# Local attention over 17 blocks of 128 keys without padding, fewer projection units, products in six steps, a new order

## The chip, the cores and the metric

The kernel runs on one core of a Trainium2 chip. Its time is the device time of one execution in microseconds (us). TensorE (PE; its weight loads are listed apart as PEld), VectorE (DVE), ScalarE (ACT) and GpSimd (POOL) compute; SyncE (SP), POOL and ACT issue transfers. Matrix products land in PSUM, eight banks of 512 fp32 columns, from which only DVE and ACT copy ("evict").

## The reference

Two branches over 2048 positions of width 640 share the input x = A_q and are mixed by a gate:

```python
g = sigmoid((x * gate_w).sum(-1, keepdims=True))
a = x * (longconv(kv, ssm_k) + kv * ssm_D)   # kv = shortconv4(A_k, shift_k) * A_v; longconv by rfft of length 4096
q, k, v = split(x @ wqkv)                    # 32 heads of width 20
b = softmax(q . k[pos - 2*w], w = 0..7) @ v, then @ wo     # 8 keys, two positions apart
out = g * a + (1 - g) * b
```

In `b` a position attends to itself and seven earlier positions of the same parity. So even and odd positions are two independent sequences of 1024 ("halves"), each with a window of 8.

## The kernel before, in words

**Order.** Everything is written as generators ("streams") that yield requests for an engine. The string `ORDER` names, character by character, whose next request is granted, and a `-` before a letter takes the second of the engines that the request allows (of "AD": ACT without, DVE with it). `Steps.run` replays this string, so it fixes the order on each engine. PSUM is handed out in the same replay (four slots of two banks, or single banks as halves). Engines run their own instructions in order and wait for each other by semaphores.

**Attention, tiles.** `xpose` transposes x into `xT` (five tiles of 128 rows; even positions, then odd, each half with padding). `vproj` makes the values of one block (`VW`, 18 blocks: 9 in each half, 114 queries and 121 keys per block, since a block needs 7 earlier keys). `qkproj` makes the queries and keys of 128 features (`ft` = 0 to 4) of all positions in *units* of five matmuls, one per tile of `xT`, into a staging tile `stg`, whose key rows are written as overlapping blocks. `fragger` moves rows of `stg` by DMA to `kb` and `qb`: four heads lie at partitions 0, 32, 64, 96, and above each head's 20 rows stand 11 rows of numbers that drive every score outside the window far below zero (`attn_consts`, `masks`). The first seven query fragments are issued by SP ("near"), the others by POOL. `NSTG` = 2 staging tiles, one for queries and one for keys, are reused by the next `ft`. Sets of four heads, t0 to t7, use three `kb`/`qb` pairs. `score_gen` makes the scores of a set in five groups of blocks, ACT takes their exponential into `ETall` (two activations a group), and `pv_gen` multiplies by the values in two parts of a set; a column of ones gives the sum, DVE takes its reciprocal and multiplies. The result `oS` lies in `VW`'s memory; `op_tr` transposes it to `oT`, and `outproj` makes 16 x 2 groups `bl`, each scaled by 1-g when it is evicted.

**Convolution.** `conv` and `conv_v` (DVE) make kv. A transform of length 4096 in two steps of products is applied to the filter (`h_stream`: tile H for half P=0 of the channels, SX for P=1) and to kv (`u_stream`, tile UC): 10 groups of the first step (evictions of 1024), then 11 of the second (`JS`, evictions of 960, the last 640). `swaps` makes a copy Hw of the transformed filter with its rows exchanged: per P four pairs of DMAs on SP, where each pair waits for the one before by way of a small POOL copy. `products(P)` multiplies on DVE, 11 steps of two; `inverse1` (20 groups of 16 matmuls) waits for all products of its P; `final` makes six groups (`TAIL`, 96 or 64 matmuls) in PSUM, evicts each by two copies into `yb`, multiplies by x*g (`load_q` loads x again and scales it) and adds `bl`; then SP stores. `load_T` and `load_wo` bring constants and the last weights on SP.

Of the kernel before, what the change touches and what calls it, by code (L numbers as in the profile page):

```python
# [13 lines left out]
ALU = mybir.AluOpType  # L14
# [12 lines left out]
BQ = 114  # L27
BK = 121
NBP = 9
NB = 2 * NBP  # L30
PRE = 7
X0 = 16
HS = 1024
HP = HS + 16
XW = X0 + 2 * HP
NF = 11
NT = 8
QW = BQ * NB
KW = BK * NB
NET = 9  # L40
GROUPS = [[0, 1, 2, 3], [4, 5, 6, 7], [8, 9, 10, 11], [12, 13, 14], [15, 16, 17]]
# [49 lines left out]
def attn_consts():  # L91
    B, C = 256.0, 512.0
    kk = np.arange(BK); qq = np.arange(BQ)
    kc = kk // 8 - 8; ko = kk % 8; qc = qq // 8 - 8; qo = qq % 8
    sk = np.where(kc % 2 == 0, 1.0, -1.0); sq = np.where(qc % 2 == 0, 1.0, -1.0)
    mk = np.zeros((NF, BK)); mq = np.zeros((NF, BQ))
# [5 lines left out]
    tot = np.einsum("fk,fq->kq", mk, mq)  # L102
    dlt = kk[:, None] - qq[None, :]
# [112 lines left out]
def kernel(  # L216
# [80 lines left out]
    xT = pL.tile([128, NDT, XW], BF, name="xT")  # L297
# [163 lines left out]
    def xdeps(i0, i1):  # L461
        return [ev(f"xT{a}") for a in range(max(0, i0) // 128, (min(HS, i1) + 127) // 128)]
# [507 lines left out]
```

## Time and profile before

| | |
|---|---|
| runs | 223.54, 224.27, 224.25 us; median 224.25 |
| the profiled execution | 224.23 us, span of its instructions 222.5 us |
| busy | PE 204.3, PEld 165.8, DVE 185.0, ACT 174.9, POOL 51.1 us |
| mean granted TensorE clock | 0.991 |

A busy time is the time in which at least one instruction of an engine runs. Matmuls overlap, so a matmul's own duration is longer than the distance to the next; a rate is read from a row that holds many of them. Four engines are busy through most of the span, so what a saved instruction is worth depends on which engine ends last in its stage.

### The profile page before, as it was taken

The page shows a single profiled execution, that of the slowest core. Times are in us where ns is not written, and L with a number is a line of the kernel's source. Part 1 is how long each engine was busy: PE and PEld are TensorE (multiplying, and loading weights), DVE is VectorE, ACT ScalarE, POOL GpSimd, SP SyncE. Part 2 cuts the span into 40 slices and gives each one's busy share as a digit, 9 for nine tenths or more (in the row PEclk, how much of TensorE's full clock was granted, in tenths as well). Part 3 has the DMA queues.
Part 4 walks back from the last instruction along what each step waited for, and adds up shares of the span by engine and source line. Part 5 has one row for each costly group of instructions (what it writes and reads, how often), then busy time and mean ns, then how long its engine had stood idle before and what let it go on. Part 6 is the DMA issues. An engine that isn't in the chain of part 4 may idle for free.

```text
span 222.5 us, 8401 instructions
## 1 busy us (share of the span) xinstructions
PE 204.3 (92%) x3577; PEld 165.8 (75%) x3577; DVE 185.0 (83%) x261; ACT 174.9 (79%) x253; POOL 51.1 (23%) x129
## 2 busy tenths in 40 slices
PE   7999999999999999699997867999999999979990
PEld 3777987696777577466685756889888899979880
DVE  4745778997998898569898978998999997859992
ACT  0264487769998898599999988998999999478770
POOL 7980711470617044402450000000000000000000
PEclk9999999999999999999999699999999999999999
DMA  6999789599999999803993396678567082003645
GB/s 199 349 237 275 188 180 205 133 168 149 208 182 197 163 151 155 140 4 52 183 171 74 85 214 152 172 174 213 122 142 227 4 184 55 3 3 91 152 106 136
DMA packets 69049, 33.35 MB, mean 150 GB/s; under 512 B 51476, under 2 KB 66708, under 8 KB 69012
## 3 DMA queue, kind: packets, MB, share of 16 engines
q1 hardware_dynamic: 65684, 27.66, 61.3%
q0 software_dynamic: 2880, 4.90, 9.9%
q8 instruction: 28, 0.46, 1.0%
q10 hardware_dynamic: 448, 0.26, 0.4%
q14 instruction: 9, 0.07, 0.1%
HBM read 19.51 MB, written 2.62 MB: 100 GB/s over the span
## 4 chain that ended last, share of the span: by engine, by line
PE 51%; DVE 20%; ACT 10%; DMA 8%; issue 7%; POOL 2%; DVEq 0%; POOLq 0%; ACTq 0%
PE PS L568 14%; PE PS L521 8%; ACT ETall L650 6%; PE PS L835 6%; DMA kb<-stg 6%; DVE UC L245 5%; PE PS L869 4%; PE PS L724 4%; PE PS L674 3%; DVE SX L245 3%; PE PS L642 3%; DVE q L926 2%; DVE yb L245 2%; ACT H L243 2%; DVE q L924 2%
## 5 line engine op out<-in xcount | busy, mean ns | idle before, releaser
L650 ACT ACTIVATE ETall<-PS 121x912 bf16<-121x912 f32 (+1 forms) x80 | 63.8, 864 | 8.1 <-PE PS L642 7.7
L568 PE MATMUL PS<-xT,Wqk 128*128 128x342 bf16 (+1 forms) x300 | 49.7, 310 | 0.6 <-ACT stg L243 0.3
L243 ACT CAST UC<-PS 128x1024 bf16<-128x1024 f32 (+2 forms) x49 | 44.4, 1030 | 4.0 <-DVE UC L245 3.1
L568 PEld LDWEIGHTS <-Wqk 128*128 128x128 bf16 x300 | 27.4, 97 | 14.3 <-issue 0.5
L521 PE MATMUL PS<-WvT,xT 128*121 128x320 bf16 x180 | 27.5, 300 | 0.1
L467 DVE TENSOR_TENSOR KX<-KX 128x1280 bf16<-128x1280 bf16 x32 | 25.3, 820 | 0.3
L618 POOL DMA_DIRECT2D qb<-stg x29 | 14.6, 506 | 45.8 <-ACT stg L243 30.5
L869 PE MATMUL PS<-wo,oT 128*128 128x320 bf16 x160 | 24.4, 302 | 0.1
L521 PEld LDWEIGHTS <-xT 128*121 128x121 bf16 x180 | 23.4, 134 | 1.4
L243 ACT CAST stg<-PS 128x363 bf16<-128x363 f32 (+1 forms) x39 | 17.1, 471 | 7.8 <-PE PS L568 7.5
L869 PEld LDWEIGHTS <-oT 128*128 128x128 bf16 x160 | 21.1, 145 | 1.5 <-issue 0.5
L724 PEld LDWEIGHTS <-G 64*128 64x128 bf16 x512 | 18.2, 93 | 4.9 <-issue 3.7
L618 POOL DMA_DIRECT2D kb<-stg x36 | 18.1, 511 | 15.8 <-ACT stg L243 7.6
L642 PE MATMUL PS<-qb,kb 31*128 31x114 bf16 x576 | 16.0, 212 | 5.1 <-DMA kb<-stg 2.3
L245 DVE CAST stg<-PS 128x342 bf16<-128x342 f32 (+1 forms) x21 | 11.0, 522 | 11.7 <-PE PS L568 9.4
L642 PEld LDWEIGHTS <-kb 31*128 31x128 bf16 x576 | 9.4, 93 | 13.5 <-issue 9.8
L674 PEld LDWEIGHTS <-ETall 121*128 121x128 bf16 x576 | 17.4, 96 | 2.1 <-issue 0.5
L674 PE MATMUL PS<-VW,ETall 121*128 121x63 bf16 (+2 forms) x576 | 18.2, 184 | 0.6 <-DVE SX L245 0.3
L835 PE MATMUL PS<-F,Hw 128*128 128x128 bf16 x160 | 18.1, 219 | 0.0
L874 ACT ACTIVATE bl<-PS,omg 128x320 bf16<-128x320 f32 x31 | 16.1, 566 | 2.4 <-PE PS L869 1.9
L835 PEld LDWEIGHTS <-Hw 128*128 128x128 bf16 x160 | 17.9, 114 | 0.0
L245 DVE CAST UC<-PS 128x1024 bf16<-128x1024 f32 x13 | 15.3, 1219 | 2.6 <-ACT UC L243 1.2
(75 smaller groups left out, 334.1 us busy)
## 6 DMA issues: line engine op xcount, KB each, us to landing
xn<-in_A_q_dram SPq DMA_DIRECT2D x8, 320.0 KB
h_lin<-in_A_ssm_k_dram SPq DMA_DIRECT2D x16, 160.0 KB
vin<-in_A_v_dram SPq DMA_DIRECT2D x8, 320.0 KB
Hw<-H SPq DMA_DIRECT2D x8, 320.0 KB
q<-in_A_q_dram SPq DMA_DIRECT2D x8, 320.0 KB
Hw<-SX SPq DMA_DIRECT2D x8, 320.0 KB
kb<-stg POOLq DMA_DIRECT2D x28, 85.1 KB, 5.5
out_dram<-q SPq DMA_DIRECT2D x16, 120.0 KB
```

What stands on the lines that cost most here:

```text
L243: nc.scalar.copy(dst, src)
L245: nc.vector.tensor_copy(dst, src)
L467: eng.tensor_tensor(d, kin[:, n + 3 - j:n + 3 - j + m, :], w.to_broadcast([128, m, QC]), ALU.mult)
L521: nc.tensor.matmul(ps[0:BK, 0:320], lhsT=xT[:, dt, s0:s0 + BK], rhs=Wv[:, dt, 320 * hp:320 * hp + 320], start=(dt == 0), stop=(dt == NDT - 1))
L568: nc.tensor.matmul(ps[:, 0:n], lhsT=Wqk[:, dt, w, 128 * ft:128 * ft + 128], rhs=xT[:, dt, s0:s0 + n], start=(dt == 0), stop=(dt == NDT - 1))
L618: (nc.sync if near else nc.gpsimd).dma_start(dst[r0:r0 + rows, 0:wd], stg[fa - f0:fb - f0, 0:wd])
L642: nc.tensor.matmul(psum(g, h4 // 2)[:, h4 % 2, BQ * bb:BQ * bb + BQ], lhsT=kb[r:r + DH + NF, BK * b:BK * b + 128], rhs=qb[r:r + DH + NF, B ...
L650: nc.scalar.activation(ETall[0:BK, e, :, 0:BQ * nb], psum(g, k)[0:BK, :, 0:BQ * nb], ACT.Exp, scale=SCALE)
L674: nc.tensor.matmul(O[:, (b - b0) // 6, c0:c0 + 21 * nh], lhsT=ETall[0:BK, e, hh, BQ * bb:BQ * bb + 128], rhs=VW[0:BK, b, 4 * t + h4:4 * t ...
L724: nc.tensor.matmul(ps[:, c, 160 * jj:160 * jj + 160], lhsT=G[rows, j0 + jj, 64 - 64 * rr:192 - 64 * rr], rhs=Am[rows, rr].rearrange("p o ( ...
L835: nc.tensor.matmul(d, lhsT=st[(key, P)][:, c, o + il // 4, :, il % 4], rhs=M[:, k, :], start=(k == 0), stop=(k == 1), skip_group_check=True)
L869: nc.tensor.matmul(op, lhsT=oT[:, ft].rearrange("p h m a -> p a (h m)")[:, t, :], rhs=wo[:, ft, 320 * n:320 * n + 320], start=(ft == 0), s ...
```

## The change

- Attention uses 17 blocks of 128 keys over the positions of both halves put end to end, without padding (2048 columns of `xT`, before 2096). A block has 120 queries, or 128 at the start of each half; block 8 crosses from the even half to the odd one, for which the mask has a form of its own, as it has for the first block. A set's last group of blocks has 2 instead of 3. `vproj` makes 17 units instead of 18, of 128 keys.
- Query units are 4 of 512 positions, key units 5 of 488 or 368, in place of 6 + 6 of 342 and 349 for each `ft`: 45 units instead of 60. A query fragment's DMA now writes each row in two pieces of 1024 elements, since `qb` has 8 columns between the halves; key fragments stay in one piece.
- `masks` takes four POOL copies a set instead of two and a memset; memsets of padding go.
- `op_tr` transposes block 8 in two pieces (18 transposes a tile, as before).
- `products` takes six steps of two instead of eleven, with 1920 elements in place of 960.
- Scaling x by g may be done by ACT too, and `final` waits for each scaled tile by itself.
- `ORDER` is another one.

```diff
-BQ = 114
-BK = 121
-NBP = 9
-NB = 2 * NBP
+BQ = 120
+BK = 128
+NB = 17
...
-GROUPS = [[0, 1, 2, 3], [4, 5, 6, 7], [8, 9, 10, 11], [12, 13, 14], [15, 16, 17]]
+GROUPS = [[0, 1, 2, 3], [4, 5, 6, 7], [8, 9, 10, 11], [12, 13, 14], [15, 16]]
+QB = [(0, 128)] + [(BQ * b + 8, BQ) for b in range(1, 8)] + [(968, 128)] + [(BQ * b + 16, BQ) for b in range(9, NB)]
+KCH = [(0, 4), (10, 3), (4, 3), (7, 3), (13, 4)]
...
 ORDER = """
-a-aa-aw-wa-aw-ww-wiiai-iiaaiaa-aia-iii-aiaa-ii-iiii-ii-iiiicifffccccw-wwww-wwwwfwwwwf-wffffwwwwwwcwcccccwwwdw-wdwddddi-wfccccccii
+a-aa-awa-a-wwww-wwwa-awaii-waiiaaa-aaaiiiiiiiiif-iiffff-iiw-wiwwwicxf-wwwwwwwwwwwwwwfxffffffcccwccwcccccc-wccffdddii-iiiidcccccccc
...
 def masks(e):
-        nc.gpsimd.memset(ksets[e][:, KW:], 0.0)
-        nc.gpsimd.tensor_copy(ksets[e][:, 0:KW].rearrange("p (b k) -> p b k", k=BK), mm[:, 0:BK].unsqueeze(1).to_broadcast([128, NB, BK]))
-        nc.gpsimd.tensor_copy(qsets[e][:].rearrange("p (b k) -> p b k", k=BQ), mm[:, BK:BK + BQ].unsqueeze(1).to_broadcast([128, NB, BQ]))
+        k_, q_ = ksets[e][:], qsets[e][:]
+        nc.gpsimd.tensor_copy(k_.rearrange("p (b k) -> p b k", k=BK), mm[:, 0:128].unsqueeze(1).to_broadcast([128, NB, BK]))
+        nc.gpsimd.tensor_copy(raw(k_, 0, [k_.ap[0], [8 * BK, 2], [1, BK]]), mm[:, 128:384].rearrange("p (a k) -> p a k", a=2))
...
 def qkproj():
-            wd, n = (BK, BQ * 3 + PRE) if w else (BQ, BQ * 3)
+            s0, n = (BQ * KCH[k][0], BQ * KCH[k][1] + 8) if w else (512 * QCH[k], 512)
+            m = BK * KCH[k][1] if w else n
...
 def fragger():
-                    g = yield Req("S", 450.0, deps, move=28.0 * rows)
+                    g = yield Req("S", 740.0, deps, move=28.0 * rows)
...
-                (nc.sync if near else nc.gpsimd).dma_start(dst[r0:r0 + rows, 0:wd], stg[fa - f0:fb - f0, 0:wd])
+                to, src = dst[r0:r0 + rows], stg[fa - f0:fb - f0]
+                if w:
+                    (nc.sync if near else nc.gpsimd).dma_start(to[:, 0:KW], src[:, 0:KW])
+                else:
+                    (nc.sync if near else nc.gpsimd).dma_start(raw(to, 0, [to.ap[0], [HS + 8, 2], [1, HS]]), src[:, 0:2 * HS].rearrange("p (a n) -> p a n", a=2))
...
+    PG = [(0, 2), (2, 4), (4, 6), (6, 8), (8, 10), (10, 11)]
...
 def products(P):
-        for k, (j0, n) in enumerate(JS):
+        for k0, k1 in PG:
+            j0 = JS[k0][0]
+            n = sum(JS[k][1] for k in range(k0, k1))
             for key in "hw":
-                r = yield Req("D", 68.0 + 0.521 * 320 * n, [ev(f"todo{P}{k}"), ev(f"hw{P}")])
+                r = yield Req("D", 68.0 + 0.521 * 320 * n, [ev(f"todo{P}{k}") for k in range(k0, k1)] + [ev(f"hw{P}")])
...
 def load_q(half):
-            r = yield Req("D", 297.0, [Ev(r.done.src, 4500.0), ev("gate")] if t == 0 else [])
-            nc.vector.tensor_scalar(q[:, t], q[:, t], g_nat[:, 8 * half + t:8 * half + t + 1], None, ALU.mult)
+            r = yield Req("DA", dict(D=297.0, A=620.0), [Ev(r.done.src, 4500.0), ev("gate")] if t == 0 else [])
+            sc = g_nat[:, 8 * half + t:8 * half + t + 1]
+            if r.eng == "A":
+                nc.scalar.activation(q[:, t], q[:, t], ACT.Copy, scale=sc)
+            else:
+                nc.vector.tensor_scalar(q[:, t], q[:, t], sc, None, ALU.mult)
```

Three places show what the new order moves. The first is ACT from the first eviction of the kv transform (UC, 128x2x512, its first step; 128x80x12 and 128x80x8 are its second) towards the first eviction of `inverse1` (128x128x8). Before:

```order
L243 CAST UC<-PS 128x2x512 x12
L243 CAST UC<-PS 128x80x12 x11
L874 ACTIVATE bl<-PS,omg 128x320 x2
L243 CAST UC<-PS 128x80x12 x3
L874 ACTIVATE bl<-PS,omg 128x320 x4
L243 CAST UC<-PS 128x80x8
L243 CAST UC<-PS 128x80x12 x2
L874 ACTIVATE bl<-PS,omg 128x320 x3
L243 CAST UC<-PS 128x80x12 x2
L874 ACTIVATE bl<-PS,omg 128x320 x2
L243 CAST UC<-PS 128x128x8
```

and ACT at the same place now:

```order
L242 CAST UC<-PS 128x2x512 x9
L242 CAST UC<-PS 128x80x12 x2
L242 CAST UC<-PS 128x2x512 x3
L242 COPY oT<-PS 128x64x2x16 x2
L242 CAST UC<-PS 128x80x12 x3
L879 ACTIVATE bl<-PS,omg 128x320
L242 CAST UC<-PS 128x80x12 x3
L879 ACTIVATE bl<-PS,omg 128x320
L242 CAST UC<-PS 128x80x12 x2
L242 CAST UC<-PS 128x80x8
L879 ACTIVATE bl<-PS,omg 128x320 x4
L242 CAST UC<-PS 128x80x12 x2
```

ACT now takes two of the five `oT` copies that were DVE's, and DVE takes five second-step evictions that were ACT's; up to the first 128x128x8 eviction ACT has 15 of 960 and two of 640 (before 18 and one) and 10 of `bl` (before 11).

The second place is DVE in the last stage, from `final`'s first group on (yb: its evictions; q: x scaled by g, the two numbers are the two halves of the positions). Before:

```order
L245 CAST yb_3616<-PS 128x2x3x160
L924 TENSOR_TENSOR q_2391<-yb_3616,q_2391 128x1920
L890 TENSOR_SCALAR q_3452<-q_3452,g_nat 128x640 x2
L926 TENSOR_TENSOR q_2391<-q_2391,bl 128x1920
L890 TENSOR_SCALAR q_3452<-q_3452,g_nat 128x640
L245 CAST yb_3616<-PS 128x2x3x160
L924 TENSOR_TENSOR q_2391<-yb_3616,q_2391 128x1920
L926 TENSOR_TENSOR q_2391<-q_2391,bl 128x1920
L890 TENSOR_SCALAR q_3452<-q_3452,g_nat 128x640 x3
L876 TENSOR_SCALAR bl<-PS,omg 128x320
```

and DVE there now:

```order
L881 TENSOR_SCALAR bl<-PS,omg 128x320
L937 TENSOR_TENSOR q_2251<-yb_3446,q_2251 128x1920
L939 TENSOR_TENSOR q_2251<-q_2251,bl 128x1920
L881 TENSOR_SCALAR bl<-PS,omg 128x320 x2
L937 TENSOR_TENSOR q_2251<-yb_3446,q_2251 128x1920
L939 TENSOR_TENSOR q_2251<-q_2251,bl 128x1920
L937 TENSOR_TENSOR q_2251<-yb_3446,q_2251 128x1280
L939 TENSOR_TENSOR q_2251<-q_2251,bl 128x1280
```

All 16 scalings now stand ahead of `final` (12 on DVE, 4 on ACT), and 11 of the 12 `yb` copies are ACT's. On PE, 75 `outproj` matmuls now stand between the first and the last group of `final`, before 95; behind the last group stand 15, before 10; and between the first group of `inverse1` and `final` stand 15 in place of 32 smaller ones of the kv transform (its second step).

The third place is SP from the first swap on (Hw; H is the filter of P=0, SX of P=1; `SX<-cf_T` is `load_T`). Before:

```order
L820 DMA Hw<-H_294 64x5x512 x2
L886 DMA q_2391<-in_A_q_dram 32x8x640
L820 DMA Hw<-H_294 64x5x512 x2
L886 DMA q_2391<-in_A_q_dram 32x8x640
L820 DMA Hw<-H_294 64x5x512 x2
L886 DMA q_2391<-in_A_q_dram 32x8x640
L820 DMA Hw<-H_294 64x5x512 x2
L820 DMA Hw<-SX 64x5x512 x2
L323 DMA wo<-in_B_wo_dram 128x5x640
L820 DMA Hw<-SX 64x5x512 x6
L323 DMA SX<-cf_T 128x4x512 x2
```

and SP there now:

```order
L322 DMA SX<-cf_T 128x4x512
L825 DMA Hw<-H_281 64x5x512 x2
L322 DMA wo<-in_B_wo_dram 128x5x640
L891 DMA q_2251<-in_A_q_dram 32x8x640 x2
L825 DMA Hw<-H_281 64x5x512 x4
L322 DMA SX<-cf_T 128x4x512
L825 DMA Hw<-H_281 64x5x512 x2
L825 DMA Hw<-SX 64x5x512 x8
L891 DMA q_2251<-in_A_q_dram 32x8x640 x2
L891 DMA q_3215<-in_A_q_dram 32x8x640 x4
```

The loads of constants and of `wo` now stand among the swaps of P=0, those of P=1 follow each other without a load between.

More of the change, by code (lines that the diff above doesn't have):

```diff
@@ L461, in xdeps @@
     def xdeps(i0, i1):
[L462 removed]
+        return [ev(f"xT{a}") for a in sorted({i // 128 % 8 for i in range(i0, i1)})]
     def taps(eng, n, m, t3, dst):
@@ L585, in qkproj @@
         for ft in range(NDT):
-            for n in range(6):
-                g = yield from unit(ft, *((n % 2, n // 2) if ft == 0 else (n // 3, n % 3)))
+            for w, k in UFIRST if ft == 0 else [(w, k) for w in range(2) for k in range(5 if w else 4)]:
+                g = yield from unit(ft, w, k)
         mark("qk", g)
```

166 lines of the change are left out of this document (83 added, 83 removed).

## The prediction, made before the change was run

> **What bounds the kernel now.** I read the page's busy times first, then cut the span at landmarks of the order.
>
> ```profile
> PE 204.3 (92%) x3577; PEld 165.8 (75%) x3577; DVE 185.0 (83%) x261; ACT 174.9 (79%) x253; POOL 51.1 (23%) x129
> ```
>
> The cuts: first transpose, first scores of t4 and t6, first `u_stream` group, first `inverse1` group, first `final` group.
>
> ```profile
> core 0: us, PE busy (x) PEld busy (x) DVE busy (x) ACT busy (x) POOL busy (x), PEclk, DMA share, GB/s
> 4.57:93.46 88.89, 86.09 (x1159) 65.44 (x1158) 71.62 (x110) 63.76 (x104) 39.95 (x97) 1.00 1.04 195
> 93.46:118.95 25.49, 24.43 (x498) 17.63 (x499) 21.34 (x28) 23.73 (x34) 7.00 (x14) 1.00 0.56 102
> 118.95:143.03 24.08, 18.84 (x496) 15.48 (x496) 20.17 (x25) 22.39 (x29) 0.57 (x3) 0.93 0.65 143
> 143.03:175.70 32.67, 32.12 (x452) 28.90 (x450) 31.47 (x43) 31.73 (x41) 0.56 (x3) 1.00 0.61 156
> 175.70:196.22 20.52, 19.38 (x356) 19.08 (x353) 17.58 (x31) 17.40 (x21) 0.00 (x0) 1.00 0.32 66
> 196.22:222.50 26.28, 20.44 (x617) 18.25 (x616) 20.23 (x26) 15.88 (x27) 0.00 (x0) 0.99 0.41 103
> ```
>
> Five stages have five different states. Up to t4 PE ends last (86.1 of 88.9; DVE 72, ACT 64). Between t4 and t6 PE and ACT are both full. Then ACT leads (22.4 of 24.1, PE 18.8). From `u_stream` on PE, DVE and ACT all fill 31 to 32 of 32.7. The last two stages are PE's, with DVE close behind and the stores at the end.
>
> **Prices on PE.** The chain of waits shows gapless runs (start, length, matmuls):
>
> ```profile
> 17.68 4.43 PE PS L568 x30
> 22.12 8.15 PE PS L521 x60
> 30.27 0.32 PE PS L642 x16
> 37.33 1.30 PE PS L674 x48
> 177.97 11.75 PE PS L835 x208
> ```
>
> A matmul of 349 columns takes 147.7 ns, one of 128 takes 56.5 ns: 0.413 ns a column and 3.7 ns fixed. A value matmul takes 136 ns, a score 20, a value product 27. Projections have 300 matmuls of 103650 columns before and 225 of 103200 now: 450 x 0.413 + 75 x 3.7 ns = 0.46 us saved. Values: 10 x 136 ns = 1.36. Scores: 32 x 20 ns = 0.64 (nothing, if their 120 to 128 columns in place of 114 cost in proportion). Value products: 32 x 27 ns = 0.87. In all 3.3 us of PE, 1.5 of it ahead of t4: there stand four fifths of the projections (0.37), one value unit of the two (0.68), and half of scores and products (0.32 and 0.43), less 0.3 for a longer first unit of `ft` 4.
>
> **Waits on fragments.** PE stops twice at scores whose key fragments are still under way:
>
> ```profile
> PE PS L642 <- DMA kb<-stg: 2.3, 2, 1.9
> 74.99 0.38 PE L642 MATMUL PS<-qb,kb 31*128 31x114 bf16 x13 [0.38 <-DMA kb<-stg]
> 91.31 0.23 PE L642 MATMUL PS<-qb,kb 31*128 31x114 bf16 x3
> 93.46 0.38 PE L642 MATMUL PS<-qb,kb 31*128 31x114 bf16 x13 [1.92 <-DMA kb<-stg]
> 87.78 5.66 DMA kb<-stg
> ```
>
> The fragment (5.66 us) cannot start before the last key unit of its `ft` is evicted, so the wait is what PE's work between that unit and the scores fails to cover. Ahead of t4 the order now has one value unit more (0.68), a query unit of 512 columns for one of 342 (0.35) and four value products fewer (0.11): 0.9 us more cover. Ahead of t3 it has one value unit, 20 value products, 12 scores and 8 filter products more and two query units of 512 for four of 342 (0.7 less): some 1.0 more. So 0.4 goes wholly and 1.0 of 1.9, rounded: 1.4 us. Bounds: 0 (the longer key unit of 488 columns and its eviction come later) to 2.3 (both gone). **Start to t4: -1.5 - 1.4 = -2.9.**
>
> **t4 to u_stream.** PE sheds 1.6 more before t6, but ACT is busy 23.7 of 25.5 there and its exponentials hold the same elements (4112 columns a set, before 4104). I take -0.4; bounds 0 and -1.6. From t6 on ACT gets one more eviction (640 of SX, DVE's before) and DVE sheds it: +0.3, bounds -0.3 and +0.7.
>
> **u_stream to final.** What ACT and DVE take apiece:
>
> ```profile
> 11.81 1.23 ACT L243 COPY xT<-PS 128x1280 bf16<-128x1280 bf16 x1
> 143.78 11.24 ACT L243 CAST UC<-PS 128x1024 bf16<-128x1024 f32 x12
> 155.83 9.87 ACT L243 CAST UC<-PS 128x960 bf16<-128x960 f32 x11 [0.81 <-ACT UC L243]
> 165.55 0.98 ACT L874 ACTIVATE bl<-PS,omg 128x320 bf16<-128x320 f32 x2
> 154.53 2.35 DVE L245 COPY oT<-PS 128x2048 bf16<-128x2048 bf16 x2
> 158.91 0.65 DVE L756 TENSOR_TENSOR Hw<-UC,Hw 128x960 bf16<-128x960 bf16 x1
> 159.48 0.65 DVE L756 TENSOR_TENSOR H<-UC,H 128x960 bf16<-128x960 bf16 x1
> 202.81 1.16 DVE L924 TENSOR_TENSOR q<-yb,q 128x1920 bf16<-128x1920 bf16 x1
> 115.62 4.35 DVE L245 CAST H<-PS 128x960 bf16<-128x960 f32 x4
> 172.39 0.48 DVE L756 TENSOR_TENSOR Hw<-UC,Hw 128x640 bf16<-128x640 bf16 x1
> ```
>
> An `oT` copy of 2048 on ACT is not in the trace: 1.23 us (the 1280 copy) and 1.97 (in proportion) bound it; I take 1.9, since the large evictions above go nearly in proportion (0.94 us for 1024). Up to the first `inverse1` eviction ACT gains two of these (3.8) and a 640 (0.6) and loses three of 960 (2.7) and one `bl` (0.5): +1.2. On DVE products of 960 follow each other at 0.57 us; a multiplication of 1920 takes 1.16 where one of 960 takes 0.65, so 0.51 more: 1.08 each, 20 x (2 x 0.57 - 1.08) = 1.2 us saved over both P (bounds: 0 at 1.14 each, 3 if the whole 0.15 us that lies beyond 960 x 0.53 ns went each time). Five evictions of 960 (1.09 each) come in, two `oT` copies (1.17) go. P=0's products, the wait that the new six steps could make longer, thus end 2 to 3 us later against `u_stream`'s start (5.4 - 2.3 - 0.6, and a `bl`); now they end at 172.9, 2.8 ahead of the first `inverse1` group. So ACT sets it: **+1.2**, bounds 0 and +2.1 (ACT's and DVE's growth on one path). Between `inverse1` and `final` PE has 15 `outproj` matmuls (2.2, from the row below) in place of 32 of the transform (1.3): **+0.9**. The scalings moved ahead lie there beside PE's 18 us of `inverse1`.
>
> **The tail.**
>
> ```profile
> 196.22 1.02 PE L912 MATMUL PS<-UC,SX 32*32 32x160 bf16 x96 [1.14 <-ACT UC L243]
> 197.17 2.94 PE L869 MATMUL PS<-wo,oT 128*128 128x320 bf16 x20
> 214.39 0.76 PE L912 MATMUL PS<-UC,SX 32*32 32x160 bf16 x64
> 217.46 0.83 DVE L926 TENSOR_TENSOR q<-q,bl 128x1280 bf16<-128x1280 bf16 x1
> ```
>
> PE goes through `final` and `outproj` without a pause, so 20 fewer of the latter between first and last group, at 0.145 us (2.87 for 20), are **-2.9**. ACT must then evict two `yb` and two `bl` per round, 2 x 0.9 + 2 x 0.5 = 2.8 of PE's 3.2 us; that just fits (bound: 0.5 lost). DVE is relieved of scalings and copies. Behind the last group PE now has 15 matmuls: 0.7 + 2.2 + an eviction 0.5 + the add 0.8 and two handovers of 0.15 make 4.5 us to the end of the last add, before 3.9 (214.39 to 218.29): **+0.6**, bounds 0.3 and 0.9.
>
> Sum: -2.9 - 0.4 + 0.3 + 1.2 + 0.9 - 2.9 + 0.6 = -3.2. The profiled execution's 224.23 us (span 222.5 and 1.7 around it; the median is 224.25) becomes **221.0**. With every bound at its better end it is -1.5 - 2.3 - 1.6 - 0.3 + 0 + 0.9 - 2.9 + 0.3 = -7.4 (216.8), at its worse end -1.2 + 0 + 0 + 0.7 + 2.1 + 0.9 - 2.4 + 0.9 = +1.0 (225.2).
>
> **Free, and why.** Mask copies on POOL (some +1 us) end well ahead of the first fragment, DVE's shorter memsets lie before its first copy waits for PE, and the two pieces of block 8 keep 18 transposes.
>
> **Rivals.** *PE is no bound, no change (0.14).* By the prices above ACT and DVE together keep their work within 1 us (what fewer units save, `oT` and scalings give back on ACT, which is slower at them), and PEld is busy only 65 of 89 us ahead of t4. If PE only looks full, -3.3 there and the covers are worth nothing, and the tail's -2.3 pays for the middle's +2.1 and +0.3: 224.3. Against it: the gapless runs above go at a fixed price per column, so PE streams. The Trainium skill says so as a rule ("Perfetto Trace Analysis", Identifying the Most-Contended Engine): matmul busy time is a bad measure of PE, weight-load share a better one. By that rule PE has a quarter in hand here and the sum would be this rival's; the row of 349 columns at 147.7 ns speaks against it.
>
> *Query fragments in two pieces, slower (0.12).*
>
> ```profile
> 21.33 5.85 SPq L618 DMA_DIRECT2D qb<-stg  x7
> 26.52 0.67 SPq L618 DMA_DIRECT2D qb<-stg  x1
> L618 POOL DMA_DIRECT2D qb<-stg x29: 499/501/533, 38.2 to 107.5; - x29
> ```
>
> SP issues seven at 0.84 us, and t0's scores follow at 30.3. If a row in two pieces costs twice at SP, t0's four fragments leave 3.3 us later; the order starts those scores 2.3 us of PE work later, while the last query unit ends some 1.5 us later, so 2.5 us of wait remain; if the landing (5.66 above) doubled too, 8, and the time is 229. It turns slower from 4.3 us on. Against it: on POOL 4 rows cost what 20 do (499 to 533 ns), and on SP the 8-row fragment, 0.67, is near the mean.
>
> *Swaps come late (0.06).* Some 1500 KB more stand ahead of P=0's last swap:
>
> ```profile
> 127.31 1.25 SPq L820 DMA_DIRECT2D Hw<-H  x2
> 144.31 8.33 DVE L245 CAST UC<-PS 128x1024 bf16<-128x1024 f32 x7
> 134.01 0.19 POOL L814 COPY Hw<-Hw 128x1 bf16<-128x1 bf16 x1 [8.48 <-DMA Hw<-H]
> 139.48 0.19 POOL L814 COPY Hw<-Hw 128x1 bf16<-128x1 bf16 x1 [5.28 <-DMA Hw<-H]
> 139.70 1.25 SPq L820 DMA_DIRECT2D Hw<-H  x2
> ```
>
> A pair takes 5.3 to 6.7 us, the longer with 320 KB beside it, so 1500 KB cost up to 6.6. The last pair lands near 145; the first product now stands behind seven of these evictions and two of 960, so at 144.31 + 8.33 + 2.2 = 154.8 in this trace's time (before: 158.3). Only beyond 9.8 us is each paid in full; twice the price gives 224.4.
>
> *More gain (0.13).* Both waits go and PE's saving counts up to t6: -2.3 for -1.4 and -1.6 for -0.4, 218.9.
>
> **Chances.** Forecast 0.55 (219.3 to 222.8), the rivals as given. 0.5% (1.1 us) is about what can be told from no change. Faster 0.72: forecast, more gain and a part of the late swaps; same 0.16: mostly the first rival; slower 0.12. The range 217.0 to 224.8 leaves out most of the second rival and the far end of the last.
>
> **What would show it.** PE's waits on `kb` at most 1 us, no new wait at t0; t4's first score 2 to 3.5 us earlier, the first `u_stream` group at about 140, `final` at about 195, its last group 16 us later; products 1.07 us apart; POOL's query issue still 0.5 us. A PE wait of over 2 us anywhere, or ACT rounds longer than PE's in the tail, would make it wrong.

## The result and the profile after: slower by 3%

The changed kernel takes 231.47 us (229.56 to 231.84), the kernel before 223.89 in the same comparison: a ratio of 1.032 (95% interval 1.026 to 1.039). The forecast was 221.0 us, range 217.0 to 224.8. Medians and ratios here and below leave out executions more than 1.5% above the fastest of their kernel, and the profiles of experiments 5, 7 and 9 are of executions left out in this way. The kernel before was run again on the chip of each group of experiments (medians 225.24, 224.46, 224.73 and 224.81).

First the profiled execution of the changed kernel (229.56 us, the shortest of four): the page's busy times, then the same cuts as before at its own landmarks (first transpose, first scores of t4 and t6, first group of the kv transform, of `inverse1`, of `final`).

```profile
PE 205.6 (90%) x3418; PEld 153.5 (67%) x3428; DVE 181.6 (80%) x233; ACT 175.5 (77%) x242; POOL 55.7 (25%) x129
```

```profile
core 0: us, PE busy (x) PEld busy (x) DVE busy (x) ACT busy (x) POOL busy (x), PEclk, DMA share, GB/s
4.56:94.95 90.39, 85.00 (x1051) 52.63 (x1057) 68.47 (x101) 61.23 (x93) 43.15 (x93) 0.98 1.06 191
94.95:119.57 24.62, 22.84 (x465) 15.39 (x467) 22.80 (x29) 23.78 (x34) 8.59 (x23) 1.00 0.64 129
119.57:146.91 27.34, 22.24 (x481) 17.97 (x480) 20.08 (x26) 23.16 (x29) 0.57 (x3) 0.69 0.67 161
146.91:180.77 33.86, 33.35 (x483) 30.10 (x482) 32.32 (x32) 32.70 (x41) 1.02 (x3) 1.00 0.48 107
180.77:202.48 21.71, 20.12 (x339) 20.00 (x336) 19.69 (x28) 20.00 (x25) 0.00 (x0) 1.00 0.31 63
202.48:227.50 25.02, 19.06 (x602) 16.36 (x601) 16.66 (x19) 14.58 (x23) 0.00 (x0) 1.00 0.42 107
```

| stage | before | after | change | forecast |
|---|---|---|---|---|
| start to t4 | 88.89 | 90.39 | +1.5 | -2.9 |
| t4 to t6 | 25.49 | 24.62 | -0.9 | -0.4 |
| t6 to the kv transform | 24.08 | 27.34 | +3.3 | +0.3 |
| to `inverse1` | 32.67 | 33.86 | +1.2 | +1.2 |
| to `final` | 20.52 | 21.71 | +1.2 | +0.9 |
| `final` to the end | 26.28 | 25.02 | -1.3 | -2.3 |

Four stages came out within about 1 us of the forecast. Two did not, and they hold 7.4 of the 8.2 us by which the span was missed (-3.2 forecast, +5.0 measured).

In the first one PE has a long pause at t2. The list of waits of the changed kernel:

```profile
DVE h_lin L778 <- DMA h_lin<-in_A_ssm_k_dram: 3.8, 1, 3.8
PE PS L642 <- DVE VW L688: 3.5, 1, 3.5
```

Its timeline there, of DVE (in brackets the pause ahead of a row and what ended it):

```profile
56.26 0.57 DVE L688 TENSOR_TENSOR VW<-PS,rd 128x400 bf16<-128x400 f32 x1
56.75 0.68 DVE L244 CAST stg<-PS 128x512 bf16<-128x512 f32 x1
61.22 0.52 DVE L778 TENSOR_TENSOR h_lin<-h_lin,Dz 128x80 bf16<-128x80 bf16 x1 [3.79 <-DMA h_lin<-in_A_ssm_k_dram]
61.43 0.45 DVE L686 RECIPROCAL rd<-PS 128x48 f32<-128x48 f32 x1
61.91 1.16 DVE L688 TENSOR_TENSOR VW<-PS,rd 128x960 bf16<-128x960 f32 x1
```

and of PE:

```profile
59.36 0.23 PE L642 MATMUL PS<-qb,kb 31*128 31x128 bf16 x2
63.13 0.39 PE L642 MATMUL PS<-qb,kb 31*128 31x128 bf16 x14 [3.54 <-DVE VW L688]
```

`h_slot` adds the D term to the loaded filter (L778) on DVE. DVE reaches that step at 57.43 and stands 3.79 us, because the load has not landed. Behind it is t1's normalisation (L686, L688), which frees the PSUM that t2's scores need, so PE stands 3.54 us. No wait for t2's own data is listed. In the order of DVE the step is now the 60th instruction, ahead of t1's first normalisation; before, it was the 71st, behind it, with one step of `conv` and two evictions between, and DVE came to it at 61.36. Two of DVE's rows before:

```profile
58.32 1.16 DVE L686 TENSOR_TENSOR VW<-PS,rd 114x960 bf16<-114x960 f32 x1
61.36 0.52 DVE L773 TENSOR_TENSOR h_lin<-h_lin,Dz 128x80 bf16<-128x80 bf16 x1
```

The load is also later. SP's rows of the changed kernel, with the near query fragments and the eight loads of the first filter half:

```profile
25.52 5.97 SPq L616 DMA_DIRECT2D qb<-stg  x7
46.94 9.81 SPq L322 DMA_DIRECT2D h_lin<-in_A_ssm_k_dram  x8
```

and before:

```profile
44.15 10.57 SPq L323 DMA_DIRECT2D h_lin<-in_A_ssm_k_dram  x8
```

The fragments, at 21.33 before, start 4.2 us later, and the loads that stand behind them on SP's queue shift by 2 to 3 us. The pause has an echo: the granted clock of the changed kernel right after it (windows of 2 us).

```profile
60.00:62.00 2.00, 0.00 (x0) 0.00 (x0) 0.75 (x3) 0.00 (x0) 0.41 (x1) 1.00 1.20 243
62.00:64.00 2.00, 0.87 (x17) 0.55 (x17) 2.00 (x3) 0.43 (x1) 0.00 (x0) 0.90 1.45 152
64.00:66.00 2.00, 2.00 (x9) 1.00 (x7) 1.37 (x3) 1.43 (x2) 0.00 (x0) 0.50 1.01 143
```

In the other stage, t6 to the kv transform, there is no long pause; the longest of PE is 1.10 us. But the mean granted clock is 0.69, before 0.93. These are two single executions: in the later comparisons the kernel before itself was granted 0.952 to 0.991 over the whole run, and its profile here has 0.991.

### The profile page after: what moved, and what is told of

Read it like the earlier page. It is cut to its first block, busy times and chain, and to the rows that moved or that the text cites. A ratio compares the mean times of both kernels' runs of the same rounds, so it can differ in the third digit from the quotient of the medians.

```text
span 227.5 us, 8049 instructions
## 1 busy us (share of the span) xinstructions
PE 205.6 (90%) x3418; PEld 153.5 (67%) x3428; DVE 181.6 (80%) x233; ACT 175.5 (77%) x242; POOL 55.7 (25%) x129
## 4 chain that ended last, share of the span: by engine, by line
PE 55%; DVE 12%; DMA 12%; ACT 7%; issue 5%; SPq 4%; POOL 2%; DVEq 0%; ACTq 0%; POOLq 0%
PE PS L564 13%; PE PS L874 10%; PE PS L676 5%; DMA qb<-stg 5%; PE PS L840 5%; DVE UC L244 4%; PE PS L517 4%; PE PS L726 4%; ACT ETall L650 4%; PE PS L642 3%; DMA h_lin<-in_A_ssm_k_dram 3%; PE PS L707 3%; DVE SX L244 3%; PE PS L925 3%; PE PS L858 2%
## 5 line engine op out<-in xcount | busy, mean ns | idle before, releaser
L650 ACT ACTIVATE ETall<-PS 128x976 bf16<-128x976 f32 (+3 forms) x80 | 63.8, 862 | 14.6 <-PE PS L642 13.3
L564 PE MATMUL PS<-xT,Wqk 128*128 128x512 bf16 (+2 forms) x215 | 47.7, 360 | 1.5 <-ACT ETall L650 0.7
L517 PE MATMUL PS<-WvT,xT 128*128 128x320 bf16 x170 | 26.4, 304 | 0.0
L642 PE MATMUL PS<-qb,kb 31*128 31x120 bf16 (+1 forms) x544 | 17.5, 229 | 6.1 <-DVE VW L688 3.5
L642 PEld LDWEIGHTS <-kb 31*128 31x128 bf16 x544 | 10.0, 98 | 18.2 <-issue 17.3
L244 DVE CAST UC<-PS 128x1024 bf16<-128x1024 f32 (+1 forms) x18 | 20.8, 1199 | 1.4 <-ACT UC L242 1.3
L517 PEld LDWEIGHTS <-xT 128*128 128x128 bf16 x170 | 16.0, 99 | 6.8 <-issue 0.3
L242 ACT CAST stg<-PS 128x512 bf16<-128x512 f32 (+1 forms) x26 | 14.2, 564 | 7.6 <-PE PS L564 6.9
L676 PEld LDWEIGHTS <-ETall 128*128 128x128 bf16 x544 | 17.8, 101 | 2.7 <-issue 1.4
L676 PE MATMUL PS<-VW,ETall 128*128 128x63 bf16 (+2 forms) x544 | 18.8, 190 | 0.8 <-DVE SX L244 0.6
L840 PE MATMUL PS<-F,Hw 128*128 128x128 bf16 x160 | 18.2, 219 | 0.0
L244 DVE CAST SX<-PS 128x1024 bf16<-128x1024 f32 (+1 forms) x12 | 14.0, 1188 | 3.4 <-PE PS L707 2.2
```

The lines of the kernel that those rows point to most:

```text
L242: nc.scalar.copy(dst, src)
L244: nc.vector.tensor_copy(dst, src)
L517: nc.tensor.matmul(ps[:, 0:320], lhsT=xT[:, dt, BQ * b:BQ * b + BK], rhs=Wv[:, dt, 320 * hp:320 * hp + 320], start=(dt == 0), stop=(dt == ...
L564: nc.tensor.matmul(ps[:, 0:n], lhsT=Wqk[:, dt, w, 128 * ft:128 * ft + 128], rhs=xT[:, dt, s0:s0 + n], start=(dt == 0), stop=(dt == NDT - 1))
L642: nc.tensor.matmul(psum(g, h4 // 2)[:, h4 % 2, QB[b][0] - q0:QB[b][0] - q0 + QB[b][1]], lhsT=kb[r:r + DH + NF, BK * b:BK * b + 128], rhs=q ...
L650: nc.scalar.activation(ETall[:, e, :, 0:nq], psum(g, k)[:, :, 0:nq], ACT.Exp, scale=SCALE)
```

## The experiments

Each line of the table is a kernel against the kernel before on the same chip.

| | edit of the changed kernel | median us | before | ratio (95%) |
|---|---|---|---|---|
| 1 | addition to h_lin late | 225.57 | 225.24 | 1.001 (0.995 to 1.007) |
| 2 | query fragments in one piece | 232.05 | 225.24 | 1.030 (1.027 to 1.033) |
| 3 | *kernel before*, addition early | 226.54 | 225.24 | 1.003 (0.997 to 1.009) |
| 4 | stage from t6 in before's order | 231.14 | 225.24 | 1.027 (1.021 to 1.032) |
| 5 | 1 and 4 | 224.75 | 224.46 | 0.999 (0.994 to 1.004) |
| 6 | 1 and filling matmuls | 224.38 | 224.46 | 1.002 (0.998 to 1.006) |
| 7 | 1 and yb copies shared | 225.46 | 224.46 | 1.002 (0.997 to 1.007) |
| 8 | 1 and before's order from t6 to the end | 223.36 | 224.73 | 0.993 (0.989 to 0.998) |
| 9 | 1 and all oT copies on DVE | 226.07 | 224.73 | 1.002 (0.997 to 1.006) |
| 10 | 8 and filling matmuls | 225.01 | 224.73 | 0.999 (0.994 to 1.003) |
| 11 | 8 and products in eleven steps | 222.74 | 224.81 | 0.990 (0.987 to 0.994) |
| 12 | 8 and filling of the filter transform | 224.44 | 224.81 | 0.996 (0.993 to 1.000) |

### 1. The addition to h_lin moved behind its load

```diff
-...-idedddleiiidiidd...-xdcexdyyyf...
+...-idedddeiiidiidd...-xdcexdlyyyf...
```

> One letter of ORDER is moved: DVE's addition to h_lin of P=0 (line 778) stands right before the first step of the filter transform, 31 requests later; the load itself and everything else stays. Theory A (DVE stands 3.8 us at that addition until the load of h_lin lands, the normalisation of t1 stands behind it, PE waits 3.54 us at t2's scores and then runs at a granted clock of 0.50 to 0.90 for 6 us): the wait goes and the clock stays at 1.0, 3.5 to 5.2 us less, median 226.3 to 228.0, t4's first score at 90 to 91.5. Theory B (query fragments in two pieces make t2 late): t2 stalls as before, median 231 to 232. Theory C (the load of h_lin is what is late, and PE only waits for it at another place): the wait moves to the first filter product on PE, median 229 to 231.

The time falls to 225.57, beside 231.14 and 232.05 of experiments 4 and 2 on the same chip: 5.6 to 6.5 us, more than the 3.5 to 5.2 that theory A had. PE goes through t2 without a pause, and the clock stays up. Rows of experiment 1, of PE (t2, t4 and t6), then of DVE, then a window right after t2:

```profile
58.93 0.39 PE L642 MATMUL PS<-qb,kb 31*128 31x128 bf16 x16
...
89.47 0.23 PE L642 MATMUL PS<-qb,kb 31*128 31x128 bf16 x3
91.10 0.38 PE L642 MATMUL PS<-qb,kb 31*128 31x128 bf16 x13 [1.40 <-DMA kb<-stg]
115.58 0.60 PE L642 MATMUL PS<-qb,kb 31*128 31x128 bf16 x16 [0.17 <-ACT H L242]
```

```profile
64.13 0.52 DVE L778 TENSOR_TENSOR h_lin<-h_lin,Dz 128x80 bf16<-128x80 bf16 x1
```

```profile
64.00:66.00 2.00, 1.99 (x33) 1.34 (x30) 2.00 (x5) 1.57 (x3) 2.00 (x5) 1.00 0.91 240
```

From t2's pause to t3 the changed kernel needs 15.17 us (63.13 to 78.30), this one 13.92 (58.93 to 72.85): so the pause costs 1.25 us beyond itself, in the stretch with the low clock. What the rest of the gain is, no run shows. Theory C is out: the wait did not move elsewhere. The first scores of t6 stand at 115.58, 3.4 us ahead of before's 118.95, where -2.9 - 0.4 had been forecast. What is left is behind t6.

### 2. Query fragments in one piece

```diff
-copy(r.eng, stg[:, s0:s0 + n], ps[:, 0:n])
+d0 = s0 + 8 * (s0 // HS)
+copy(r.eng, stg[:, d0:d0 + n], ps[:, 0:n])
+if s0 == HS:
+    copy(r.eng, stg[:, HS:HS + 8], ident[:, 0:8])
...
-dma_start(raw(to, 0, [to.ap[0], [HS + 8, 2], [1, HS]]), ...)
+dma_start(to[:, 0:QW], src[:, 0:QW])
```

> The queries are staged with the gap of 8 columns, so each row of a query fragment is one piece of 2056 elements; five copies of 8 columns are added. Theory A (h_lin): no change beyond 1 us, median 230.5 to 232, although POOL's query issue falls from 0.59 to 0.50 us and SP's from 0.85 to near 0.84. Theory B (two pieces): 2.5 to 4 us less, median 227.5 to 229, and the stall at t2 gone or under 1.5 us.

POOL's issue is back at its old price (in the changed kernel it is 594 ns), the time is not. Rows of experiment 2, from its page and from PE's timeline:

```profile
L619 POOL DMA_DIRECT2D qb<-stg x29 | 14.5, 505 | 40.4 <-DVE stg L244 17.9
```

```profile
63.76 0.59 PE L645 MATMUL PS<-qb,kb 31*128 31x128 bf16 x14 [4.63 <-DVE VW L691]
```

The two pieces cost 0.09 us an issue on an engine that has time. Theory B is out.

### 3. The kernel before, with the addition early

```diff
-...ifxdddxedidff...icddlie-iiiyf...
+...ifxdddxeldidff...icddie-iiiyf...
```

> The kernel before, with one letter of its ORDER moved: the addition to h_lin of P=0 (line 773) stands ahead of the normalisation of t1's first part, as in the changed kernel, and not three steps behind it. Theory A: DVE stands there from about 57.8 us until the load lands near 61, the scores of t2 wait 1.5 to 3.5 us, and the granted clock may fall behind it: median 225.5 to 229. Theory C (only the lateness of the load in the changed kernel matters) and B: the load is there in time, median 223.5 to 224.5.

Theory A holds for PE's wait (2.05 us) and the median (226.54, which the ratio of 1.003 cannot tell from before); but DVE stands from 55.9 and the load is there at 57.8, not near 61. DVE, PE and a window of experiment 3:

```profile
57.83 0.52 DVE L773 TENSOR_TENSOR h_lin<-h_lin,Dz 128x80 bf16<-128x80 bf16 x1 [1.94 <-DMA h_lin<-in_A_ssm_k_dram]
```

```profile
62.08 0.38 PE L642 MATMUL PS<-qb,kb 31*128 31x114 bf16 x14 [2.05 <-DVE VW L686]
93.31 0.39 PE L642 MATMUL PS<-qb,kb 31*128 31x114 bf16 x16
```

```profile
62.00:64.00 2.00, 1.93 (x53) 1.54 (x56) 1.75 (x5) 1.48 (x2) 0.14 (x1) 1.00 1.22 233
```

This gives the account of the slack. With before's queue on SP the load lands at 57.8, and before's DVE came to it at 61.36: 3.5 us in hand. The change moved DVE's step 3.9 us ahead (57.43) and the landing back by 3.4 us (61.2) or more (DVE's wait was 3.8, 4.9 and 6.2 us in the changed kernel and in experiments 2 and 4; in the last two the trace names the next load on SP's queue, G, which this step does not read, so that `h_lin` landed by then is inferred). Worked out from these, the first move alone would have made DVE wait 0.4 us (57.43 to 57.8), the second alone none (61.2) to 2.4 (61.36 to 63.8). It also shows how the kernel before can bear such a pause: in this execution, the shortest of four (224.51 us, the others 226.5 to 228.4), two us of it are taken back at t4, where the 1.92 us wait for a key fragment is gone, and the span is 222.7 (before 222.5). The clock stayed at 1.00 after a pause of 2.05 us.

### 4 and 5. The stage from t6 in the order of before

```diff
-dzjdddd-zz-zdddz-zzd-zczzdddzc-zzzzzz-zzzedddjddze-zzdd-zdz-zjddjeeddz-zddpdejdddezzz-zzzzzeezzz-zzzooq
+djddddz-zzd-zdddz-zzzz-zzcczz-zzzzzz-zeddddeddzdd-zeddjjdezdddd-zz-zz-zjddedddzedzz-zzzeezzz-zzpzz-zjooq
```

> The changed kernel, with the grants from t6's first scores to the first group of the kv transform in the order of the kernel before (the same 91 grants; of the filter transform, 30 of scores and 8 of value products). Theory D (the new order of this stage lets PE, DVE and ACT wait for each other by turns, and the granted clock falls to 0.50 for some 18 us, the stage takes 27.3 instead of 24.1 us): the stage returns to 24 to 25 us and a granted clock of 0.9 or more, median 228.3 to 229.5. Theory E (the clock falls in this stage whatever the order, by what went before): the stage stays above 26.5 us, median 230.5 to 232.

> The changed kernel with the addition to h_lin late (as in the first experiment) and the stage from t6 to the kv transform in the order of before (as in the fourth). Theory D (order of that stage): the two gains add, that stage falls from 28.0 to about 25 us; of it the next stage gives back 1.3 us as it did alone; median 223.5 to 225.0, against 225.6 with the late addition alone. Theory E (the granted clock falls there whatever the order): stage 27 to 28 us, median 225.5 to 227.

By the stage, experiment 4 speaks for theory D (24.89 us) and 5, with the same order in it, does not (26.85). By the medians it is the other way about: 231.14 in 4 lies in theory E's range, 224.75 in 5 in theory D's, and the profile of 5 is of the longest of its twelve executions (228.62 us). So neither theory is shown. That stage in 4, and in 5:

```profile
122.92:147.81 24.89, 19.45 (x481) 15.79 (x480) 19.75 (x23) 22.65 (x29) 0.56 (x3) 0.86 0.66 161
```

```profile
117.30:144.15 26.85, 22.50 (x480) 18.02 (x480) 19.98 (x23) 22.57 (x29) 0.56 (x3) 0.68 0.72 173
```

The longer stage is the one with the lower granted clock (0.86, 0.68), and the clock is not set by the order alone. In both the next stage takes 35.2 us, 1.3 more, for a reason that no run shows. In the time nothing is gained: 0.999 of before, with the late addition alone 1.001.

### 6. Filling PE

```diff
+for n in range(4 if t >= 6 else 0):             # ahead of a group of scores
+    nc.tensor.matmul(psum(g, 0)[:, 0, 0:128], lhsT=ident[:], rhs=ident[:], start=True, stop=True, ...)
+for n in range(4 if key == "h" and P else 0):   # ahead of a first-step group
+    nc.tensor.matmul(ps[:, 0, 0:128], lhsT=ident[:], rhs=ident[:], start=True, stop=True, ...)
```

> The changed kernel with the late addition, and four additional matmuls of 128 columns with a full array (0.22 us, results overwritten) ahead of each of the 10 groups of scores of t6 and t7 and of the 10 first-step groups of the P=1 filter transform: 4.5 us more of PE work in a stage where PE idles 5 of 28 us. Theory F (the granted clock falls because PE does little there, and the low clock is what makes the stage long): clock of the stage 0.9 or more instead of 0.63, stage 25 to 26.5 us, median 223 to 225. Theory G (PE, DVE and ACT hand over to each other by turns, the clock is only a companion): the added work lies on the path, stage 29 to 32 us, median 227 to 229.

The stage in experiment 6, and, for comparison, in experiment 1 (the longest of its four executions):

```profile
115.80:142.43 26.63, 23.00 (x558) 17.75 (x557) 19.92 (x25) 23.04 (x29) 0.57 (x3) 1.00 0.62 151
```

```profile
115.58:143.60 28.02, 23.02 (x480) 18.69 (x480) 20.13 (x26) 23.28 (x29) 0.56 (x3) 0.63 0.66 163
```

4.5 us more work on PE, and the stage is 1.4 us shorter. Theory G, by which the stage gets longer, is out: the low clock is a cause of its length and not only a companion. The whole run's clock was 0.993 to 1.000 in all 12 executions (experiment 1: 0.948 to 0.978). In the whole time no gain can be told: 1.002 of before, 1.001 without filling.

### 7. Sharing the yb copies

```diff
-...tttts-sstsssttttts-ss-...
+...ttt-ts-sstssstttt-ts-ss-...
```

> The changed kernel with the late addition, and the second yb copy of each group of the last stage on DVE instead of ACT (five copies; the sixth group's pair already has one there). Theory H (PE waits in the last stage for the second of two copies that ACT makes one after the other, 1.82 us, some 0.3 us a round): first to last group of that stage 15.5 us instead of 16.4, median 0.6 to 1.0 us below that of the late addition alone. Rival (DVE is full there too, 16.7 of 25 us, and its copies stand ahead of its multiplications): no gain, the last group at the same time within 0.3 us.

There is no gain, as the rival said (in its profile the last group even comes 0.8 us later, not within 0.3). PE's rows of the last stage in experiment 7 (two of the rounds):

```profile
206.76 0.84 PE L874 MATMUL PS<-wo,oT 128*128 128x320 bf16 x5 [0.25 <-DVE bl L881]
212.46 0.84 PE L874 MATMUL PS<-wo,oT 128*128 128x320 bf16 x5 [0.19 <-DVE bl L881]
213.52 0.57 PE L925 MATMUL PS<-UC,SX 32*32 32x160 bf16 x42 [0.23 <-DVE yb L244]
```

PE now waits for DVE, and from the first to the last group it takes 17.0 us, without the edit 16.2.

### 8. Before's order from t6 to the end

The changed kernel's string up to t6 (with edit 1), and from there the string of before, with every other pair of products and two grants of `fragger` left out and four grants of `gate` put ahead, as the counts need it.

> The changed kernel up to t6 (with the late addition to h_lin) and, from t6's first scores to the end, the order of the kernel before, with the products still in six steps. Theory D' (what is left of the loss is the new order behind t6): the stages return to before's, 24.1 to 25 us to the kv transform, 32.7 to inverse1 (or up to 1.2 less for the six steps), 20.5 to the last stage and 26.3 from there, 103.5 in all behind t6 at 115.8: span 219.3, median 221 to 222.5, and with what the new blocks save ahead of t6 faster than both kernels. Rival E' (the new blocks or the granted clock make the stage behind t6 long in any order): that stage 26.5 us or more, median 223.5 to 225.

Faster than both kernels: 0.993 (0.989 to 0.998). With the late addition alone it was 1.001, so by the medians the order behind t6 cost some 1.7 us beyond the pause at t2 (the intervals overlap); about 1 us of it lies outside the span of the instructions (an execution lasts 1.8 us beyond its span here and 2.9 in experiment 1, by the medians). But 223.36 us lies between the two forecasts, and the stages did not all return to before's: the profiled run has 26.03, 33.44, 20.51 and 26.46 us, 106.4 in all where 103.5 was expected; the first again at a low clock (0.74), the second 0.8 over before for a reason that no run shows.

### 9. All oT copies on DVE

```diff
-...1-1r-rrrr-rrrr-r000...
+...1-1r-rr-rr-rr-rr-r000...
```

> The changed kernel with the late addition, and all five oT copies on DVE instead of three (two copies of 1.9 us less on ACT, two of 1.17 more on DVE). The reason given in the prediction (ACT's added work sets the stage from the kv transform to inverse1): the stage falls from 33.9 to 32 to 33 us, median 0.8 to 1.8 below the late addition alone. Rival (PE sets it: busy 33.4 of 33.9 us there, by the filter or kv matmuls that were moved into it): the stage stays at 33.5 to 34.2 us, median unchanged within 0.8.

By the stage neither; in the time the rival holds, with no gain (1.002, without the edit 1.001). The stage from the kv transform to `inverse1` in experiment 9:

```profile
142.33:177.27 34.94, 33.59 (x484) 30.11 (x482) 34.41 (x34) 29.35 (x39) 1.14 (x3) 1.00 0.44 98
```

ACT is relieved by 3.4 us and the stage gets 1.1 us longer, with DVE busy 34.4 of it. ACT did not set it alone; DVE, at 32.3 of 33.9 before the edit, had no room.

### 10 and 12. Filling with the order of before

The same lines as in experiment 6, with 2 instead of 4 in experiment 10; with 4, ahead of the first-step groups alone, in experiment 12.

> The kernel of the eighth experiment (the order of before behind t6), with two additional full-array matmuls of 128 columns (0.11 us) ahead of each of the 10 score groups of t6 and t7 and of the 10 first-step groups of the P=1 filter transform. Theory F (the low granted clock itself costs time there): clock of the stage at 0.95 or more and the stage 0.5 to 1.0 us shorter than without, median 220.5 to 222. Theory G (the clock is only a companion): the 2.2 us of added work show, stage 0.5 to 2 us longer, median 222 to 224.

> The kernel of the eighth experiment, with four additional full-array matmuls of 128 columns (0.22 us) ahead of each of the 10 first-step groups of the P=1 filter transform only, 2.2 us in all. Theory F (the granted clock falls because PE does little from t6 on, and the low clock costs time): granted clock of the stage at 0.95 or more, stage 24.5 to 25.5 us instead of 26.0, median 221.8 to 223.2. Rival (the scores' stretch starts the fall, and filling the transform alone does not prevent it): clock 0.70 to 0.85, stage 26 to 27.5 us, median 223.5 to 225.

The stage in the profiled execution of 10, then of 12:

```profile
115.08:140.43 25.35, 21.03 (x521) 15.75 (x519) 20.36 (x25) 22.50 (x29) 0.57 (x3) 1.00 0.53 119
115.99:142.45 26.46, 22.69 (x520) 17.78 (x520) 20.44 (x26) 22.86 (x29) 0.56 (x3) 0.87 0.57 130
```

Without filling it was 26.03 us at 0.74. But the profile of 10 is of the shortest of its twelve executions (222.50 us). Over the whole run the clock was 0.980 to 0.998 in five of them (222.5 to 225.3 us) and 0.954 to 0.969 in seven (225.2 to 228.2 us): two matmuls at each place keep the clock up only at times, where four, in experiment 6, did in all twelve. Within this one kernel, then, the time goes with the clock. Theory F's stage came in the profile, its median (220.5 to 222) did not: 225.01. In 12 the rival holds (stage and median; the clock, 0.87, is a little above its range). In time neither gains: 0.999 and 0.996 of before, without filling 0.993.

### 11. Products in eleven steps again

```diff
-    PG = [(0, 2), (2, 4), (4, 6), (6, 8), (8, 10), (10, 11)]
+    PG = [(k, k + 1) for k in range(11)]
```

> The kernel of the eighth experiment, with the products in eleven steps of two again, where the kernel before has them. The prediction (six steps save DVE 0.6 us ahead of inverse1 and 1.2 in all, but another engine sets that stage): the stage from the kv transform to inverse1 33.2 to 33.6 us as with six steps, DVE busy 0.6 us more there, median within 0.5 of the eighth experiment's 223.4. Rival (a step that waits for two groups of the kv transform starts later and is what makes this stage 33.4 instead of 32.7 us): 32.6 to 32.8 us, 0.7 less. Rival (DVE's saved time is on the path): 34.0 us or more.

The stage takes 33.45 us, with six steps 33.44: the six steps are worth nothing on the path of this stage, as the prediction said. This is the best version that ran, 222.74 us, 0.990 (0.987 to 0.994) of before; the interval overlaps with that of experiment 8, so that eleven steps are better is not shown. The cuts of experiment 11 at the same landmarks:

```profile
4.56:114.16 109.60, 105.74 (x1514) 66.87 (x1522) 92.06 (x129) 84.92 (x127) 51.77 (x115) 1.00 0.99 182
114.16:139.62 25.46, 21.44 (x481) 17.32 (x480) 20.36 (x26) 22.68 (x29) 0.56 (x3) 0.73 0.63 143
139.62:173.07 33.45, 32.92 (x452) 29.04 (x451) 31.65 (x43) 31.73 (x41) 0.56 (x3) 1.00 0.59 147
173.07:193.58 20.51, 19.36 (x354) 19.07 (x352) 17.52 (x30) 17.39 (x21) 0.00 (x0) 1.00 0.32 66
193.58:219.80 26.22, 20.45 (x617) 18.27 (x616) 20.23 (x26) 15.87 (x27) 0.00 (x0) 0.99 0.41 103
```

## Why the prediction was wrong

**Start to t4 (-2.9, measured +1.5): the step that failed is a wait that was not looked for.** The savings were there. In six kernels that hold the new attention with the late addition (1, 6, 8, 10, 11, 12), t6 starts at 114.2 to 116.6, on the mean 115.5, so 3.4 us ahead of before, and -3.3 had been forecast for both stages. What the text left out is the consumer of a load. It did see that the last query unit ends later ("some 1.5 us"; SP's first fragment went out 4.2 us later) and followed that only as far as t0's scores, which indeed did not stop (they start at 32.42, with no wait listed). What stands behind those fragments on SP, the filter load, and DVE's step that waits for it, now 3.9 us ahead, had no term. The signal that the text named, "a PE wait of over 2 us anywhere", is what appeared. The pause and the clock behind it make 3.5 + 1.25 us, which more than covers the 4.4 us of error.

**The waits on fragments (-1.4).** No PE wait for `kb` is left in the changed kernel, but it came late to t4. With the late addition that wait was 1.40, 0.43, 1.06, 0.19, 0.23 and 1.11 us in the same six kernels, which have one order up to there. The landing of one fragment varies by over 1 us, and the term was a draw from that.

**t6 to the kv transform (+0.3, measured +3.3): mis-sized, because the forecast counted work of ACT and DVE and took PE for free.** Their busy times hardly moved (ACT +0.8, DVE -0.1); PE's clock did, and had no term. The stage by order and mean granted clock:

| order | length us (clock) |
|---|---|
| before's: before, 3, 4, 11, 8 | 24.08 (0.93), 24.43 (0.86), 24.89 (0.86), 25.46 (0.73), 26.03 (0.74) |
| new: changed, 2, 1 | 27.34 (0.69), 27.37 (0.69), 28.02 (0.63) |

From 0.93 to 0.73 or 0.74 before's order loses 1.4 to 2.0 us, so some 8.5 us for each whole unit of clock. At 0.69 it would take 26.1; the new order takes 27.3. By that estimate, of the 3.3 us some 2 go with the clock and 1.2 with the order itself. That the clock is a cause is shown by experiment 6; what starts each fall, and why the same order gets 0.86 once and 0.73 another time, is not. In the profile of before the fall stood already (0.93), and the prediction passed it by; since before's own clock varies as much from run to run, a part of the 3.3 us may be the draw of two executions. The Trainium skill ("TensorE: Matmul & The Clock Gate", "HAM oscillation — how this bites in real kernels") says that gaps of PE beyond about 3.4 us bring the clock down: here it fell after 3.54 and did not after 2.05. Its next section ("A second HAM failure mode: psum-queue depth-cycling") has it fall by many small gaps too, in a kernel that cycles through PSUM banks. In this stage no gap is above 1.10 us; whether the cause is the same, no run shows.

**kv transform to inverse1 (+1.2, measured +1.2): right in size, the reason not shown.** ACT was named; experiment 9 takes ACT's share away and gains nothing. The `oT` copy on ACT, 1.9 by estimate, takes 1.87; products follow each other at 1.07 us, as worked out.

**inverse1 to final (+0.9, measured +1.2)** held; but the scalings on ACT, said to lie beside PE, stand in the chain that ends last. Its row in the changed kernel:

```profile
196.52 2.27 ACT q L898 x3
```

**The tail (-2.9 and +0.6, measured -1.9 and +0.9).** First to last group takes 16.3 us (202.48 to 218.77). The forecast named 16 as the sign, but its term of -2.9 from before's 18.2 makes 15.3, so the 20 matmuls do not count in full. PE now stands inside groups of `final`, for which the trace names no engine; two such rows, and the last add:

```profile
215.97 0.68 PE L925 MATMUL PS<-UC,SX 32*32 32x160 bf16 x54 [0.28 <-issue]
219.70 0.25 PE L925 MATMUL PS<-UC,SX 32*32 32x160 bf16 x5 [0.22 <-issue]
222.75 0.82 DVE L939 TENSOR_TENSOR q<-q,bl 128x1280 bf16<-128x1280 bf16 x1
```

"That just fits" was wrong by 1 us. That it is ACT's copies for which PE stands is likely, but not shown: experiment 7 gives five of them to DVE and gains nothing. From the last group to the end of the last add it is 4.8 us, before 3.9; the stores behind it take 0.3 less.

**The rivals.** Two pieces: refuted by experiment 2, though POOL's issue did rise to 0.59 us, against the forecast 0.5. Late swaps: no wait of the products for them is listed. "PE is no bound": refuted ahead of t6, where PE's savings and the shorter waits were to be worth nothing by it and came to 3.4 us; and with it, for this stretch, the reading that the weight-load share leaves PE a quarter in hand. The rival that came true, a load's consumer moved ahead of its load, was not on the list.

## What to carry to other kernels

When an order changes, list every instruction that waits for a load, and for each reckon anew when its engine reaches it and when the load can land, with all that is queued ahead of it; here 3.5 us of slack went because both ends moved. Judge a hand-made order by stages: putting the old order back behind t6 and moving one letter turned 1.032 into 0.993. And a stage where PE is a fifth idle isn't free on PE: look at the granted clock there before counting on the other engines alone, and at that of all executions, not of the profiled one only: in experiment 10 it had 0.998, seven others 0.954 to 0.969.

## What the runs showed of the hardware

- A pause of PE of 3.54 us was followed by a granted clock of 0.90 and 0.50 in the next two windows of 2 us, one of 4.63 us (experiment 2) by 0.67, 0.50 and 0.50, one of 2.05 us (experiment 3) by 1.00.
- Matmuls whose results are thrown away can shorten a stage: with 4.5 us of them it took 26.6 us at a clock of 1.00 (experiment 6), without them 28.0 at 0.63 (experiment 1).
- The granted clock varies from run to run of one kernel: 0.954 to 0.998 over the whole run in experiment 10, 0.952 to 0.991 in the kernel before.
- Two pieces for a row instead of one raise the issue of a DMA on POOL from 505 to 594 ns.
- The time of an execution beyond its span is 1.7 to 1.9 us for the kernel before and the kernels that end in its order (but for one execution of experiment 8, 3.0), and 2.0 to 3.6 us in those that end in the new one, save experiments 6 (1.8 in all) and 7 (mostly 1.8). It is up to 1.5 us of the loss in the changed kernel; where it is spent no profile here shows.
